# W_ch1 is loaded as bf16 by a casting DMA from the GpSimd queue

## The chip, the cores and the metric

The kernel runs on one core of a Trainium2 chip. A core has engines with an instruction queue each: TensorE (PE, matrix products), VectorE (DVE), ScalarE (ACT), GpSimd (POOL) and SyncE (SP, which here only issues DMAs). Sixteen DMA engines move data between the chip's memory (HBM) and the on-chip buffer (SBUF). Matrix products land in PSUM, which has eight banks. An engine runs its own queue in order; order between engines is made by semaphores only.

The metric is the device time of one execution in microseconds (us). All times inside an execution are given from the start of its span, that is from its first instruction.

## What is computed

```python
kv  = einsum('bhsd,bhse->bhde', k, v)          # 8 batches, 8 heads, 576 rows, 64 columns
o   = einsum('bhsd,bhde->bhse', q, kv)
x   = o / sqrt(mean(o*o, -1) + 1e-6) * g_norm  # heads side by side: x is (8, 576, 512)
a1  = alpha1 * x + beta1
tok = einsum('ts,bsd->btd', w_tok, a1)
u   = x + lam * tok
a2  = alpha2 * u + beta2
ch  = maximum(a2 @ w_ch1, 0) @ w_ch2           # 512 -> 2048 -> 512
out = u + lam * ch
```

All inputs and the output are fp32 in HBM. `w_ch1` is 512 x 2048 and `w_ch2` 2048 x 512, 4 MiB each.

## The kernel before

Every piece of work is first recorded by `P.op(queue, cost, function, r=reads, w=writes)`. `Prog.schedule` then runs the recorded operations through a small planner in Python, with the costs written beside each one, and so fixes the order of each queue; `synchronize` derives the semaphore waits from the reads and writes, and `emit` writes the program. So an edit to one operation, its queue or its planned cost can reorder work on every engine. Two queue names stand for one engine in `queue_of`: "AQ" is a DMA issued from ScalarE's queue.

One batch goes through these stages. Rows of a batch are cut into four chunks of 128 (c0 to c3) and a tail of 64; two batches share one chunk of tails.

- `load_kv`, `load_q` (L324, L330): k, v and q into `kf`, `vf`, `qf`, 1 MiB each, and three tails of 128 KiB. SP issues them, two batches ahead, each as soon as its buffer has been read.
- `round_kv`, `permute_q` (L347, L351, L355): VectorE rearranges them into `kr`, `vr`, `krt`, `vrt`, `qr`.
- `kv_groups` (L366, L369 on TensorE, L389 and L392 to `kvc`) and `qt_groups` (L407, then L414/L420 to `qt`).
- `qkv_groups`, per chunk: L451 (TensorE), the square L459 and root L464 on ScalarE, and on VectorE the sum L461, the reciprocal L467, the product L471 to `xm` (this one frees the chunk's PSUM), L476 to `rt` (bf16) and L480.
- `tok_groups`, per chunk: L496 (TensorE, five matmuls, it needs all five `rt`), L502 (VectorE, adds to `xm`), and two GpSimd operations in a row, L506 to `a1f` and L509 to `a2b`. There is one buffer `a1f`.
- `ut_groups`: transposes L527 of two chunks at a time, and the copy L533 to `a2t` (ScalarE).
- `ch1_groups`: `a2t` times `w1`, L560 on even batches (64 matmuls) and L575 on odd ones (128, with the tails), then the relu L551 to `ht` (ScalarE).
- `ch2_groups`: `ht` times `w2`, L597, then L606 (VectorE) and the store.

The weights are prepared once. `w_tok` goes through L674 and L679 to `wt`. `load_w(i)` for i = 0 to 3 brings a quarter of `w_ch1` into a slot of the fp32 staging buffer `stg` (three slots of 1 MiB) by SP's queue and casts it to bf16 on ScalarE into `w1` (L736); i = 4 to 7 brings a quarter of `w_ch2` into `stg` and multiplies it by `lam` into `w2`, half of it on VectorE and half on GpSimd (both L746). The first four are recorded ahead of batch 0's `qkv_groups`, the last four after batch 1's loads.

Of the kernel before, what the change touches and what calls it, by code (L numbers as in the profile page):

```python
# [10 lines left out]
ACT = mybir.ActivationFunctionType  # L11
# [11 lines left out]
class Op:  # L23
# [3 lines left out]
    def __init__(self, eng, cost, fn, pri, idx):  # L27
        self.eng, self.cost, self.fn, self.pri, self.idx = eng, cost, fn, pri, idx
        self.deps, self.raw = set(), set()
        self.alloc, self.tiles = [], []  # L30
        self.start = self.end = self.pos = None
        self.waits, self.inc, self.lat, self.clock, self.sem = [], False, 0.0, None, None
# [15 lines left out]
class Prog:  # L48
# [5 lines left out]
    def __init__(self, nc, stack):  # L54
        self.nc, self.stack = nc, stack
        self.ops, self.lastw, self.readers = [], {}, {}
        self.ps = stack.enter_context(nc.psum_tensor("ps", [128, 8, 512], F32))
        self.eng = {"PE": nc.tensor, "ACT": nc.scalar, "DVE": nc.vector,
                    "POOL": nc.gpsimd, "SP": nc.sync, "AQ": nc.scalar}
        self.bias = 0  # L60
        self.pe_window = 8

# [112 lines left out]
        self.sequence = sorted(self.ops, key=lambda o: (o.start, o.idx))  # L175

    def queue_of(self, e):
        return "ACT" if e == "AQ" else e

    def synchronize(self):  # L180

# [64 lines left out]
def bass_transnormer_attn__then__resmlp_affine_kernel(  # L246
# [15 lines left out]
    with ExitStack() as stack:  # L262
        P = Prog(nc, stack)

        def sb(name, shape, dt):
            return stack.enter_context(nc.sbuf_tensor(name, shape, dt))
# [14 lines left out]
        qf = sb("qf", [128, NH, 4, DH], F32)  # L281
# [8 lines left out]
        stg = sb("stg", [128, 3, 4, 512], F32)  # L290
# [12 lines left out]
        w1 = sb("w1", [128, 4, FF], BF16)  # L303
# [9 lines left out]
        def dve_us(n, mode=1):  # L313
            return 0.17 + n / 960.0 / mode

        def act_us(n):
            return 0.19 + n / 1200.0
# [269 lines left out]
        def ch2_groups(b):  # L587
# [31 lines left out]
            for c, n in order:  # L619
# [8 lines left out]
            w=["wst"], dma_us=3.0)  # L628
# [3 lines left out]
            w=["wst2"], dma_us=0.5)  # L632
        P.op("SP", 0.6, lambda e: e.dma_start(wst2[0:64, 256:832], moe_w_tok[512:576, :]),
             w=["wst3"], dma_us=0.5)
        for src, dst, key in ((moe_lam, lam_bc, "lam"), (moe_alpha1, e1_bc, "e1"),
# [10 lines left out]
             w=["identb"])  # L646
# [62 lines left out]
        def run(gens):  # L709
            for gen in gens:  # L710
# [14 lines left out]
             r=["wtp"] + [("wtm", i) for i in range(6)], w=["wt", ("sm", 3)])  # L725
# [4 lines left out]

        def load_w(i):
            if i < 4:
                P.op("SP", 0.6, lambda e: e.dma_start(
                    stg[:, i % 3], moe_w_ch1[:, 512 * i:512 * i + 512].rearrange(
                        "(j p) f -> p j f", p=128)), w=[("stg", i % 3)], dma_us=3.2)
                P.op("ACT", act_us(2048), lambda e: e.activation(  # L736
                    w1[:, :, 512 * i:512 * i + 512], stg[:, i % 3], ACT.Identity),
                    r=[("stg", i % 3)], w=[("w1", i)], pri=100)
            else:
                n = i - 4  # L740
                P.op("SP", 0.6, lambda e: e.dma_start(
                    stg[:, i % 3], moe_w_ch2[512 * n:512 * n + 512, :].rearrange(
                        "(j p) c -> p j c", p=128)), w=[("stg", i % 3)], dma_us=3.2)
                for hh in range(2):
                    P.op("POOL" if hh else "DVE", dve_us(1024) * (1 + hh),
                         lambda e, hh=hh: e.tensor_tensor(  # L746
                        out=w2[:, 4 * n + 2 * hh:4 * n + 2 * hh + 2, :],
                        in0=stg[:, i % 3, 2 * hh:2 * hh + 2, :],
                        in1=lam_bc[:, None, :].to_broadcast([128, 2, DM]), op=ALU.mult),
                        r=[("stg", i % 3), "lam"], w=[("w2h", n, hh)])  # L750
                P.lastw[("w2", n)] = P.lastw[("w2h", n, 0)] + P.lastw[("w2h", n, 1)]

        for i in range(4):
            load_w(i)
# [3 lines left out]
        for i in range(4, 8):  # L758
            load_w(i)
# [67 lines left out]
```

## Time and profile before

| what | before |
|---|---|
| time, median of 3 runs | 423.66 us (423.46 to 424.52) |
| the profiled execution: its time | 423.83 us |
| the profiled execution: its span | 422.0 us |
| TensorE busy | 376.5 us (89% of the span), mean granted clock 0.964 |
| VectorE, ScalarE, GpSimd busy | 226.8, 167.5, 120.3 us |
| HBM read, written | 39.37 MB, 9.44 MB |
| ScalarE casts of `w_ch1` (L736) | 4, of 1.90 us each |
| GpSimd multiplications by `lam` (L746) | 4, of 2.35 to 3.32 us |
| VectorE multiplications by `lam` (L746) | 4, of 1.21 to 1.27 us |

The profile is one execution, taken by the hardware profiler. Its page gives the busy time of each engine, the span in 40 slices with the busy share of each in tenths, the chain of work that ended last, and the costliest groups of instructions by line. The same trace can be asked for the instructions in order of time and for the busy times in any stretch. "PEld" is TensorE's loading of weights, "PEclk" the granted TensorE clock as a share of full speed.

### The profile page before, as it was taken

What the parts mean: (1) busy time and instruction counts of PE and PEld (TensorE: products, weight loads), DVE (VectorE), ACT (ScalarE), POOL (GpSimd) and SP (SyncE); (2) the same over time, 40 slices, a digit from 0 to 9 for tenths busy, and PEclk for the clock granted to TensorE, in tenths of its full rate; (3) what the DMA queues carried; (4) which work ended last, traced back from release to release, by engine and by line L of the source; (5) the groups of instructions that cost most, each with busy time, mean ns of one, the idle gap of its engine ahead of it and who ended that gap; (6) DMA issues with size and microseconds to landing.
All of it is one profiled execution on the core that took longest, in us unless ns stands there. A gap on an engine that the chain in (4) does not pass through costs nothing.

```text
span 422.0 us, 5398 instructions
## 1 busy us (share of the span) xinstructions
PE 376.5 (89%) x2193; PEld 227.8 (54%) x2193; DVE 226.8 (54%) x371; ACT 167.5 (40%) x263; POOL 120.3 (29%) x92
## 2 busy tenths in 40 slices
PE   0574755899899999999999999999999999999994
PEld 0563242444677465545775565446774665446642
DVE  3439894995587336862786165743783228620011
ACT  1069142540477025712673135503770157215600
POOL 1000499309300830038003800074007400290000
PEclk9985695999999999999999999999999999999999
DMA  8999999202293019501670139001100201011012
GB/s 241 331 349 302 359 265 351 84 0 99 71 282 85 2 75 263 125 1 61 214 163 2 50 124 284 6 26 51 37 2 0 76 25 25 2 50 51 2 50 75
DMA packets 49128, 49.15 MB, mean 116 GB/s; under 512 B 14608, under 2 KB 39184, under 8 KB 49104
## 3 DMA queue, kind: packets, MB, share of 16 engines
q1 hardware_dynamic: 46672, 46.29, 37.7%
q10 hardware_dynamic: 2432, 2.52, 1.9%
q8 instruction: 17, 0.28, 0.3%
q14 instruction: 7, 0.06, 0.0%
HBM read 39.37 MB, written 9.44 MB: 116 GB/s over the span
## 4 chain that ended last, share of the span: by engine, by line
PE 69%; POOL 12%; DVE 7%; DMA 4%; ACT 3%; issue 2%; POOLq 0%; SPq 0%
PE ps L597 22%; PE ps L575 17%; PE ps L560 12%; POOL a1f L506 6%; POOL a2b L509 6%; PE ps L496 6%; PE ps L451 4%; PE ps L407 4%; DMA qf<-in_q_dram 4%; PE ps L366 2%; PE ps L527 1%; DVE xm L480 1%; DVE xm L502 1%; DVE krt L351 1%; PE ps L674 1%
## 5 line engine op out<-in xcount | busy, mean ns | idle before, releaser
L597 PE MATMUL ps<-w,ht 128*128 128x512 bf16 x576 | 135.3, 379 | 0.0
L506 POOL TENSOR_TENSOR a1f<-xm,a_bc 128x512 f32<-128x512 f32 x32 | 42.8, 1337 | 255.3 <-DVE xm L502 253.5
L551 ACT ACTIVATE ht<-ps 128x640 bf16<-128x640 f32 (+1 forms) x96 | 77.8, 810 | 50.2 <-PE ps L560 25.3
L597 PEld LDWEIGHTS ps<-w,ht 128*128 128x128 bf16 x576 | 54.1, 98 | 57.0 <-DVE xm L502 0.6
L575 PE MATMUL ps<-a2t,w 128*128 128x320 bf16 x512 | 73.0, 299 | 0.0
L606 DVE TENSOR_TENSOR xm<-ps,xm 128x512 f32<-128x512 f32 x32 | 22.1, 690 | 83.1 <-PE ps L597 83.0
L533 ACT ACTIVATE a2t<-ps 128x1024 bf16<-128x1024 bf16 (+1 forms) x20 | 18.8, 938 | 116.8 <-PE ps L527 116.8
L560 PE MATMUL ps<-a2t,w 128*128 128x512 bf16 x256 | 61.2, 388 | 2.6 <-ACT a2t L533 1.1
L575 PEld LDWEIGHTS ps<-a2t,w 128*128 128x128 bf16 x512 | 48.7, 98 | 19.9 <-ACT a2t L533 0.3
L509 POOL TENSOR_TENSOR a2b<-a1f,b_bc 128x512 bf16<-128x512 f32 (+1 forms) x40 | 54.2, 1355 | 3.1
L496 PE MATMUL ps<-rt,wt 128*128 128x512 bf16 x200 | 46.9, 393 | 7.5 <-DVE rt L476 7.5
L560 PEld LDWEIGHTS ps<-a2t,w 128*128 128x128 bf16 x256 | 23.8, 100 | 30.4 <-issue 1.8
L366 PE MATMUL ps<-vr,kr 128*128 128x256 f32 x128 | 26.5, 332 | 13.8 <-DVE vrt L351 13.8
L496 PEld LDWEIGHTS ps<-rt,wt 128*128 128x128 bf16 x200 | 20.0, 100 | 32.5 <-DVE rt L476 7.8
L451 PE MATMUL ps<-kvc,qt 128*128 128x256 f32 x160 | 33.2, 338 | 2.7 <-ACT kvc L392 2.7
L461 DVE TENSOR_REDUCE small<-sq 128x8 f32<-128x512 f32 (+1 forms) x40 | 27.1, 677 | 11.4 <-ACT sq L459 11.3
L502 DVE TENSOR_TENSOR xm<-ps,xm 128x512 f32<-128x512 f32 x32 | 22.0, 690 | 16.9 <-PE ps L496 16.7
L366 PEld LDWEIGHTS ps<-vr,kr 128*128 128x128 f32 x128 | 20.3, 206 | 16.9 <-DVE vrt L351 14.3
L451 PEld LDWEIGHTS ps<-kvc,qt 128*128 128x128 f32 x160 | 25.7, 210 | 6.8 <-ACT kvc L392 3.0
L414 ACT ACTIVATE qt<-ps 128x1024 fp32r<-128x1024 f32 x16 | 16.4, 1024 | 22.3 <-PE ps L407 22.3
L480 DVE SCALAR_TENSOR_TENSOR xm<-e_bc,wsum,xm 128x512 f32<-128x512 f32 x32 | 25.0, 782 | 0.2
L459 ACT ACTIVATE sq<-ps 128x512 f32<-128x512 f32 (+1 forms) x40 | 23.6, 591 | 2.9 <-PE ps L451 2.8
(57 smaller groups left out, 294.6 us busy)
## 6 DMA issues: line engine op xcount, KB each, us to landing
kf<-in_k_dram SPq DMA_DIRECT2D x8, 1024.0 KB, 7.4
qf<-in_q_dram SPq DMA_DIRECT2D x8, 1024.0 KB, 9.6
stg<-in_moe_w_ch_dram SPq DMA_DIRECT2D x8, 1024.0 KB, 10.8
out_dram<-xm SPq DMA_DIRECT2D x32, 256.0 KB, 2.3
vf<-in_v_dram SPq DMA_DIRECT2D x7, 1024.0 KB, 9.0
vf<-in_v_dram ACTq DMA_DIRECT2D x1, 1024.0 KB, 9.8
kft<-in_k_dram SPq DMA_DIRECT2D x8, 128.0 KB, 9.3
qft<-in_q_dram SPq DMA_DIRECT2D x8, 128.0 KB, 9.0
```

The source lines that it names most:

```text
L366: e.matmul(o, flat(kr[:, c, 2 * pr:2 * pr + 2, :]), flat(vr[:, c, u0:u0 + 4, :]), start=(c == 0), stop=False)
L451: m = e.matmul(t.flat()[:, 256 * pr:256 * pr + 256], qt[:, pr, 128 * c:128 * c + 128], kvc[:, pr, :], start=True, stop=True)
L461: P.op("DVE", dve_us(512), lambda e: e.tensor_reduce(out=small[rows, sms], in_=sq[rows, sqs], axis=AX.X, op=ALU.add), r=[("sq", sqs)], w=[ ...
L480: P.op("DVE", dve_us(560), lambda e: e.scalar_tensor_tensor(out=x, in0=e2_bc[rows, :], scalar=wsum[rows, wc:wc + 1], in1=x, op0=ALU.mult, ...
L496: m = e.matmul(t.flat(), wt[:, ws, col:col + 128], rt[:, sc, :], start=(sc == 0), stop=(sc == 4))
L502: P.op("DVE", dve_us(512), lambda e: e.tensor_tensor(out=x, in0=t.flat(rows), in1=x, op=ALU.add), r=[t, xkey(b, c)], w=[xkey(b, c)], pri=-100)
L506: P.op("POOL", pool_us(512), lambda e: e.tensor_tensor(out=a1f[rows, af, :], in0=x, in1=a2_bc[rows, :], op=ALU.mult), r=[xkey(b, c), "a2"] ...
L509: P.op("POOL", pool_us(512), lambda e: e.tensor_tensor(out=a2b[rows, c, :], in0=a1f[rows, af, :], in1=b2_bc[rows, :], op=ALU.add), r=[("a1 ...
L551: P.op("ACT", act_us(n), lambda e: e.activation(dst, src(), ACT.Relu), r=[t], w=key)
L560: m = e.matmul(t.ap()[:, i, :], w1[:, dj, 128 * (fj + i):128 * (fj + i) + 128], a2t[:, dj, 0:512], start=(dj == 0), stop=(dj == 3))
L575: m = e.matmul(t.ap()[:, i, 0:320], w1[:, dj, 128 * fj:128 * fj + 128], a2t[:, dj, 320 * i:320 * i + 320], start=(dj == 0), stop=(dj == 3))
L597: m = e.matmul(t.flat(), ht[:, fj, 128 * c:128 * c + 128], w2[:, fj, :], start=(fj == 0), stop=(fj == 15))
```

## The change

`load_w` for the first four quarters no longer uses `stg` and ScalarE. One DMA, issued from GpSimd's queue under the new name "GQ", reads the fp32 quarter from HBM and writes it as bf16 into its place in `w1`. It is recorded as a reader of `qf`, so it waits until batch 0's q has landed, and batch 1's load into `qf` waits for it. The quarters of `w_ch2` now take the staging slots in the order 0, 1, 2, 0.

```diff
     def queue_of(self, e):
-        return "ACT" if e == "AQ" else e
+        return {"AQ": "ACT", "GQ": "POOL"}.get(e, e)
...
             if i < 4:
-                P.op("SP", 0.6, lambda e: e.dma_start(
-                    stg[:, i % 3], moe_w_ch1[:, 512 * i:512 * i + 512].rearrange(
-                        "(j p) f -> p j f", p=128)), w=[("stg", i % 3)], dma_us=3.2)
-                P.op("ACT", act_us(2048), lambda e: e.activation(
-                    w1[:, :, 512 * i:512 * i + 512], stg[:, i % 3], ACT.Identity),
-                    r=[("stg", i % 3)], w=[("w1", i)], pri=100)
+                P.op("GQ", 1.0, lambda e: e.dma_start(
+                    w1[:, :, 512 * i:512 * i + 512], moe_w_ch1[:, 512 * i:512 * i + 512].rearrange(
+                        "(j p) f -> p j f", p=128)), r=["qf"], w=[("w1", i)], dma_us=3.2)
             else:
                 n = i - 4
                 P.op("SP", 0.6, lambda e: e.dma_start(
-                    stg[:, i % 3], moe_w_ch2[512 * n:512 * n + 512, :].rearrange(
-                        "(j p) c -> p j c", p=128)), w=[("stg", i % 3)], dma_us=3.2)
+                    stg[:, n % 3], moe_w_ch2[512 * n:512 * n + 512, :].rearrange(
+                        "(j p) c -> p j c", p=128)), w=[("stg", n % 3)], dma_us=3.2)
                 for hh in range(2):
                     P.op("POOL" if hh else "DVE", dve_us(1024) * (1 + hh),
                          lambda e, hh=hh: e.tensor_tensor(
                         out=w2[:, 4 * n + 2 * hh:4 * n + 2 * hh + 2, :],
-                        in0=stg[:, i % 3, 2 * hh:2 * hh + 2, :],
+                        in0=stg[:, n % 3, 2 * hh:2 * hh + 2, :],
                         in1=lam_bc[:, None, :].to_broadcast([128, 2, DM]), op=ALU.mult),
-                        r=[("stg", i % 3), "lam"], w=[("w2h", n, hh)])
+                        r=[("stg", n % 3), "lam"], w=[("w2h", n, hh)])
```

The planner, run on the changed list, gives these new orders. GpSimd's queue: the four DMAs, then three of its multiplications by `lam`, then batch 0's L506/L509 pairs, then the fourth multiplication. SP's queue: the first three quarters of `w_ch2` stand where three quarters of `w_ch1` stood; the fourth follows batch 1's k, v and tails; batch 1's q comes only after batch 2's k and v. VectorE: one multiplication by `lam` ahead of the last `rt` of batch 0, one behind it, one after L502 of chunk c1. TensorE: batch 1's L407 and the L451 of its chunks c0 to c3 stand behind batch 0's L560 instead of ahead of it and between; 40 of batch 0's 64 L597 stand ahead of batch 1's L496 instead of 16. From batch 1's first L575 on, the same work is left as before, in nearly the same order.

More of the change, by code (lines that the diff above doesn't have):

```diff
@@ L58, in __init__ @@
         self.eng = {"PE": nc.tensor, "ACT": nc.scalar, "DVE": nc.vector,
-                    "POOL": nc.gpsimd, "SP": nc.sync, "AQ": nc.scalar}
+                    "POOL": nc.gpsimd, "SP": nc.sync, "AQ": nc.scalar, "GQ": nc.gpsimd}
         self.bias = 0
```

## The prediction

> **What bounds the kernel now.** I read the page's slices first, then the busy times by stretch, then the chain of waits in order of time, then single instructions.
>
> ```profile
> PE   0574755899899999999999999999999999999994
> ...
> POOL 1000499309300830038003800074007400290000
> PEclk9985695999999999999999999999999999999999
> DMA  8999999202293019501670139001100201011012
> ```
>
> Each digit is 10.55 us. TensorE is full from the eighth slice on; only the first seven (to 74 us) have room. There the DMA engines are full too, and the granted clock falls to half. GpSimd is idle in slices two to four.
>
> ```profile
> 32.00:45.00 13.00, 5.23 (x22) 4.03 (x22) 12.51 (x27) 9.73 (x14) 0.00 (x0) 0.53 1.12 303
> ...
> 116.00:160.00 44.00, 44.00 (x286) 28.40 (x286) 25.12 (x42) 18.99 (x33) 12.66 (x10) 1.00 0.42 109
> ```
>
> Columns: stretch, length, busy us of PE, PEld, DVE, ACT, POOL, clock, DMA share, GB/s. From 116 us TensorE is at 44.00 of 44.00. From 32 to 45 us the full engine is VectorE, 12.51 of 13.00, and not ScalarE with the casts.
>
> ```profile
> 37.36 1.80 ACT w L736
> ...
> 58.10 0.67 DVE xm L502
> ...
> 59.40 2.23 POOL a1f L506
> 61.63 0.06 POOL w L746
> 61.69 3.18 issue
> 64.87 2.25 POOL a2b L509
> ...
> 67.17 1.05 PE ps L527 x8
> ...
> 69.32 3.61 PE ps L560 x8
> ```
>
> The chain (start, us, what) shows one cast of L736 in it, and further on what holds batch 0's first L560: L502 of chunk c3, then GpSimd's L506, a multiplication by `lam` (L746, 61.6 to 64.9) and L509.
>
> The first L575 of batch 1 starts at 115.94. The work behind it is the same in both kernels, so the end moves as this mark moves: 423.83 (profiled time; 1.83 of it lies outside the span of 422.0) plus the shift. 423.83 is 0.17 above the median. I sum the shift in four steps.
>
> **Step 1, the start of batch 0's L496 (45.09).** The change takes four casts of 1.90 us off ScalarE, 7.6 us. Three lie between 32.9 and 41.8 on the way to `rt`. But VectorE idles 0.49 of those 13 us, so the gain is between 0 and 0.5; I take the one idle stretch of 0.28 that ends with ScalarE's L459. The fourth cast (46.9) has no waiter. Against it, VectorE now makes a multiplication (1.13 from start to next start) ahead of the last `rt` and one L480 (0.73) less: +0.40. Together +0.1.
>
> Then a new collision. GpSimd now multiplies three times between about 31 and 46, where it did nothing.
>
> ```profile
> 54.72 1.76 DVE L480 SCALAR_TENSOR_TENSOR xm<-e_bc,wsum,xm 128x512 f32<-128x512 f32 x1
> ...
> 72.92 4.68 POOL L746 TENSOR_TENSOR w<-stg,lam_bc 128x1024 bf16<-128x1024 f32 x2
> ...
> 75.10 2.78 DVE L351 CAST krt<-kft 64x512 fp32r<-64x512 f32 x1
> ```
>
> A cast of 0.41 us took 2.78 beside a multiplication on GpSimd, an L480 of 0.74 took 1.76 beside L506 and L509. The other way, GpSimd's L506 grew from 1.27 to 2.23 beside VectorE's multiplication. So operations that read SBUF twice, or copy it, exclude GpSimd's. L476, five on this path, has two SBUF inputs like L480. No row shows L476 beside GpSimd. Three multiplications of 2.35: the cost is 0 if each falls on operations with a PSUM input (L502 kept 0.67 beside GpSimd), 7.05 if each holds VectorE whole. I take half, 3.5. Step 1: +3.6.
>
> The DMAs on GpSimd's queue are new. Four issues stand ahead of those multiplications. SP's issues took 0.37 with room and 5.88 (vf at 22.25) without. At 5.88 four end at 18.34 + 23.5 = 41.9, three multiplications at 48.9, against 48.22 for the first L506: 0.7 late, hidden because L502 of c3 decides. So 0 for the issue; above 8 us each it decides. The Trainium skill, "DMA: Bandwidth & Descriptors", section "Anatomy of one DMA — SWDGE (gpsimd) path", calls descriptor generation small and the fixed part of a transfer about 2 us; by it the multiplications would start when `stg` lands and the sum would stay.
>
> **Transfers.** The bytes read stay the same, and the DMA share is 1.0 or more from 4 to 66 us, so only the order moves. Batch 1's k and v now share the engines with seven quarters instead of standing between them. A quarter takes 2.7 us at the 385 GB/s of 46 to 50 us; `w_tok`'s last part landed at 24.2; seven quarters end near 43, kf near 46.5 and vf near 50 at 3.3 each, the tails near 51. VectorE wants them at 52 and later: 0, with some 2 us of cover on vf and 5 on kf. `w1` is wanted at 69, a cover of 26. Batch 1's q now waits on SP behind batch 2's k and v and for all four `w1` DMAs, with only batch 3's k and v due behind it; issued at about 58 + 3.5, landing 10 later (9.8 before) and rearranged by 76, it meets an L407 due at 82: 0.
>
> **Step 2, L496 to L502 of c3.** Before, 13.0 (45.09 to 58.10), 4.49 of it up to L502 of c1. After L502 of c1 the new VectorE order has L502 0.60, multiplication 1.13, kr 1.21, L480 0.73, vr 1.73, L502 0.60, krt 0.81, vrt 0.34, two L480 at 1.69: 10.5 by the durations of this stage. Sum 15.0, so +2.0. Bounds: kr at its 2.31 beside GpSimd adds 1.1; L480 and vr undisturbed take off 2.4.
>
> **Step 3, L502 of c3 to L560.** Before 11.2. The multiplication (61.6 to 64.9, 3.24) is gone from between L506 and L509, and so is VectorE's beside L506. With L502 0.70, L506 and L509 at their usual 1.27 and gaps of 0.1, L527 0.62 and L533 1.03 it is 5.1; with this stage's long ones 8.0. VectorE's next work is L389, with a PSUM input, so I stay near the short end: 5.6, that is -5.6. L560 then starts at 69.3.
>
> **Step 4, L560 to L575.** Before 46.6. After, TensorE makes 64 L560 (0.217 each, 13.9), 16 L407 (1.7), 20 L451 (2.4), 40 L597 (8.6), 26.6 in all, before batch 1's L496. The late L451 cost cover: c3 needs the PSUM that L471 of c0 frees, and square, two sums, reciprocal and product (0.6, 1.3, 0.2, 0.7 and the root 0.3) end 2.35 after TensorE is done with c2; L597 then waits 0.9 for L471 of c1, or 3.7 for c2's. Stalls 3.25 to 6.05; I take 4. Batch 1's `rt` are ready about when the 40 L597 end. From L496 on GpSimd decides: 1.09, L502 0.70, five pairs 13.5, L527 0.40, L533 0.60, 16.4 to 17.0 (before 23.0, bound by TensorE). 30.6 + 16.7 = 47.3: +0.7. The old stage held 2.5 us of half clock (eight L560 in 3.60 and not 1.73, L451 1.42 and not 0.82). Its idle gap was 7.2 us; the new one is near 3.5, and before, the clock fell about 3.8 us into the gap. I charge half, 1.25. Step 4: +2.0.
>
> **Sum.** 3.6 + 2.0 - 5.6 + 2.0 = +2.0, so 425.8.
>
> One rule speaks against the change: the Trainium skill, "SBUF — State Buffer", section "SBUF: two separate sides", says that descriptors from GpSimd's queue can't be written while VectorE runs a two-port copy, and blames stalled DMAs on that. No row here has such a DMA. The copies around the issues are qr (18.34, 1.23 us) and few more until 45; by the rule the `w1` loads start some 1.2 later, and the sum stays, given their cover.
>
> **Rivals.**
> - *GpSimd's multiplications miss VectorE* (other side). For it: most of VectorE's work from 32 to 45 reads PSUM or one SBUF tile. Against: five L476 in 12 us. Place: step 1; price 3.5; with it the gap before L560 shrinks and the clock stays up, 1.25. 425.8 - 4.75 = 421.1. With the clock up, it is faster by over 0.3% when the collisions stay under 1.5 us in all.
> - *Half of both*: one multiplication collides (2.35) and the clock stays up: 425.8 - 1.15 - 1.25 = 423.4, no change that can be told.
> - *The casting transfer takes the engines twice as long a byte.* No row shows one. SP's transfers then run at a third of their pace until about 52: `stg`'s third slot near 53, vf near 60 against a wanted 57.5. L502 of c3, and the end with it, move by some 3: 429. At four times, `w1`'s last quarter comes after 70 and batch 1's q behind it: 436 and more. Against: the packets written are still 1 KiB rows like k's, which moved at about 300 GB/s.
>
> **How the numbers follow.** Forecast 0.42, first rival 0.27, second 0.15, third 0.16. A difference under 0.3% (1.3 us) can't be told from none; 0.05 of the forecast's low end lies there. So faster 0.27, same 0.20, slower 0.53. The range takes in the first rival and the third's near price with some 2 us of step 4's upper stall: 420.8 to 431.0. The forecast's own range is 424 to 428.5.
>
> **What would show it.** L736 gone; L476 or L480 of batch 0 at 1.7 or more beside L746 on GpSimd; L496 near 48.7; L560 near 69 at full clock; L575 near 118. TensorE waiting for `w1` or VectorE for kf would show the third rival; L476 all at 0.68 the first. I am wrong most if GpSimd's four issues take over 8 us each, or if batch 1's q is late.

## The result and the profile after

| | time, median | ratio to the kernel before, 95% interval |
|---|---|---|
| before | 424.09 us | |
| after | 429.33 us (426.76 to 429.77) | 1.0111 [1.0068, 1.0155] |

Both medians are of four executions. The change makes the kernel 1.1% slower. The profiled execution of after took 429.55 us, its span is 427.7. In a second comparison the same program gave 429.77 us and a ratio of 1.0174 [1.0140, 1.0209], because before was a little quicker there (422.72). So the size of the ratio is uncertain by half a per cent from one comparison to the next; its sign is not.

First the slices of the page, as they were read for before (each digit is 10.7 us now):

```profile
PE   0572556979989999999999999999999999999994
...
POOL 1224277002920560019101910065006500190000
PEclk9977666989999999999999999999999999999999
DMA  8999965911196016801490029201100201011012
```

From the eighth slice on (75 us) TensorE is again nearly full but for a dip in the ninth; where the loss lies is read from the marks further down. GpSimd now works in slices two to four, where it was idle. The low clock is still there.

The second view is the chain of waits of after, in order of time (start, us, what), cut to its main pieces:

```profile
39.16 2.81 DVE rt L476
...
45.81 1.13 DVE w L743
...
48.00 3.38 PE ps L496 x9
...
53.14 2.29 DVE kr L347
55.43 1.67 DVE xm L480
...
63.87 0.67 DVE xm L502
...
69.59 12.70 PE ps L560 x47
...
84.50 1.75 PE ps L407 x16
...
94.31 8.44 PE ps L597 x37
102.75 1.09 PE ps L496 x5
...
116.12 2.15 POOL a1f L506
...
118.34 2.15 POOL a2b L509
...
121.79 2.17 PE ps L575 x16
```

L736 and the multiplication between L506 and L509 are gone from it. In their place stand an L476 of 2.81, a multiplication on VectorE (L743, 45.81), then 47 L560 in one block with batch 1's L407 behind them, and at the end L506 and L509 at 2.15 each.

The marks of the prediction, for every kernel that ran (us from the start of the span; "b1" is batch 1; the column L560 to L575 is the difference of its two marks):

| kernel | L496 | L502 c3 | first L560 | L496 b1 | first L575 b1 | L560 to L575 | span | span less L575 |
|---|---|---|---|---|---|---|---|---|
| before | 45.09 | 58.10 | 69.32 | 92.98 | 115.94 | 46.62 | 422.0 | 306.1 |
| after | 48.00 | 63.87 | 69.59 | 102.59 | 121.63 | 52.04 | 427.7 | 306.1 |
| after, again | 48.31 | 64.31 | 69.86 | 102.46 | 121.51 | 51.65 | 427.6 | 306.1 |
| 1: q not held | 48.13 | 65.27 | 70.67 | 92.08 | 113.91 | 43.24 | 420.0 | 306.1 |
| 2: GpSimd late | 45.13 | 61.12 | 67.09 | 97.75 | 119.66 | 52.57 | 425.7 | 306.0 |
| 3: both | 44.02 | 61.16 | 66.56 | 91.08 | 111.15 | 44.59 | 417.3 | 306.2 |
| 3 again | 43.16 | 60.71 | 65.87 | 90.62 | 110.70 | 44.83 | 416.8 | 306.1 |
| 4: 3, VectorE late too | 43.29 | 56.91 | 63.59 | 94.79 | 117.28 | 53.69 | 423.4 | 306.1 |
| 5: before, GpSimd late | 42.79 | 55.80 | 63.33 | 88.89 | 111.03 | 47.70 | 417.1 | 306.1 |
| 6: before, both late | 44.29 | 57.31 | 63.01 | 92.33 | 112.40 | 49.39 | 418.5 | 306.1 |

The last column is the same for all of them: from batch 1's first L575 on, every one of these kernels takes 306.1 us. All that differs has happened by then. In after the mark moved by 5.69 us and the span by 5.7.

### The profile page after: what moved, and what is told of

Its sections match the earlier page's. It is cut to its first block, busy times and chain, and to the rows that moved or that the text cites. A ratio compares the mean times of both kernels' runs of the same rounds, so it can differ in the third digit from the quotient of the medians.

```text
span 427.7 us, 5367 instructions
## 1 busy us (share of the span) xinstructions
PE 374.5 (88%) x2161; PEld 227.4 (53%) x2193; DVE 231.5 (54%) x371; ACT 160.6 (38%) x259; POOL 122.7 (29%) x96
## 3 DMA queue, kind: packets, MB, share of 16 engines
q1 hardware_dynamic: 44560, 42.10, 34.1%
## 4 chain that ended last, share of the span: by engine, by line
PE 70%; POOL 13%; DVE 7%; DMA 4%; issue 3%; ACT 2%; POOLq 0%; SPq 0%
PE ps L597 23%; PE ps L575 16%; PE ps L560 13%; POOL a2b L509 6%; POOL a1f L506 6%; PE ps L496 6%; PE ps L451 4%; DMA qf<-in_q_dram 4%; PE ps L407 4%; PE ps L366 2%; DVE rt L476 1%; PE ps L527 1%; DVE xm L502 1%; DVE xm L480 1%; PE ps L674 1%
## 5 line engine op out<-in xcount | busy, mean ns | idle before, releaser
L597 PE MATMUL ps<-w,ht 128*128 128x512 bf16 x554 | 133.1, 381 | 1.5 <-issue 0.2
L506 POOL TENSOR_TENSOR a1f<-xm,a_bc 128x512 f32<-128x512 f32 x32 | 42.0, 1312 | 230.2 <-DVE xm L502 228.5
L597 PEld LDWEIGHTS ps<-w,ht 128*128 128x128 bf16 x576 | 54.3, 98 | 58.0 <-issue 1.1
L575 PE MATMUL ps<-a2t,w 128*128 128x320 bf16 x512 | 73.0, 299 | 0.0
L560 PE MATMUL ps<-a2t,w 128*128 128x512 bf16 x251 | 60.7, 391 | 1.7 <-ACT kvc L392 1.5
L575 PEld LDWEIGHTS ps<-a2t,w 128*128 128x128 bf16 x512 | 48.7, 98 | 19.9 <-ACT a2t L533 0.6
L496 PE MATMUL ps<-rt,wt 128*128 128x512 bf16 x195 | 44.8, 387 | 13.3 <-DVE rt L476 13.1
L509 POOL TENSOR_TENSOR a2b<-a1f,b_bc 128x512 bf16<-128x512 f32 (+1 forms) x40 | 53.9, 1349 | 3.1
L560 PEld LDWEIGHTS ps<-a2t,w 128*128 128x128 bf16 x256 | 24.3, 100 | 30.0 <-issue 3.4
L496 PEld LDWEIGHTS ps<-rt,wt 128*128 128x128 bf16 x200 | 19.8, 99 | 36.9 <-DVE rt L476 12.9
L451 PE MATMUL ps<-kvc,qt 128*128 128x256 f32 x160 | 30.8, 320 | 4.5 <-ACT kvc L392 2.5
L502 DVE TENSOR_TENSOR xm<-ps,xm 128x512 f32<-128x512 f32 x32 | 22.1, 690 | 17.0 <-PE ps L496 16.9
L366 PEld LDWEIGHTS ps<-vr,kr 128*128 128x128 f32 x128 | 21.4, 217 | 17.2 <-DVE vrt L351 14.6
L451 PEld LDWEIGHTS ps<-kvc,qt 128*128 128x128 f32 x160 | 23.6, 195 | 8.3 <-ACT kvc L392 2.7
L480 DVE SCALAR_TENSOR_TENSOR xm<-e_bc,wsum,xm 128x512 f32<-128x512 f32 x32 | 25.8, 805 | 0.2
L476 DVE TENSOR_TENSOR rt<-xm,e_bc 128x512 bf16<-128x512 f32 x32 | 25.0, 783 | 0.3
```

Source lines behind the costliest of these rows:

```text
L366: e.matmul(o, flat(kr[:, c, 2 * pr:2 * pr + 2, :]), flat(vr[:, c, u0:u0 + 4, :]), start=(c == 0), stop=False)
L451: m = e.matmul(t.flat()[:, 256 * pr:256 * pr + 256], qt[:, pr, 128 * c:128 * c + 128], kvc[:, pr, :], start=True, stop=True)
L476: P.op("DVE", dve_us(512), lambda e: e.tensor_tensor(out=rt[rows, c, :], in0=x, in1=e1_bc[rows, :], op=ALU.mult), r=[xkey(b, c), "e1"], w= ...
L480: P.op("DVE", dve_us(560), lambda e: e.scalar_tensor_tensor(out=x, in0=e2_bc[rows, :], scalar=wsum[rows, wc:wc + 1], in1=x, op0=ALU.mult, ...
L496: m = e.matmul(t.flat(), wt[:, ws, col:col + 128], rt[:, sc, :], start=(sc == 0), stop=(sc == 4))
L506: P.op("POOL", pool_us(512), lambda e: e.tensor_tensor(out=a1f[rows, af, :], in0=x, in1=a2_bc[rows, :], op=ALU.mult), r=[xkey(b, c), "a2"] ...
```

## The experiments

The theory after the result: the casting DMA costs nothing and gains nothing. What the edit changes is the order, by two routes. The first is the record that the DMAs read `qf`: batch 1's q load has to wait for them, SP issues it behind batch 2's k and v, and the planner, which expects q late, puts batch 1's L407 and L451 behind batch 0's L560. The second is that GpSimd's three multiplications by `lam` run early, beside VectorE's work for batch 0. The rival is that the transfer itself does the harm, by its load on the DMA engines or by its issue.

The trace of after speaks against the rival. Its DMA queues (packets, MB, share of 16 engines' time; q0 is the casting queue, whose MB are those written) are:

```profile
q1 hardware_dynamic: 44560, 42.10, 34.1%
q0 software_dynamic: 2112, 2.10, 2.9%
```

2.9% of 427.7 us is 12.4 us of all sixteen engines for the 4.19 MB that the four DMAs read, 338 GB/s; the plain queue takes 145.8 us for 42.10 MB, 289 GB/s. The same 4.19 MB, moved by the plain queue in before, made up about 13.3 us of its time (37.7% of 422.0 us for 46.29 MB there, 145.8 us for 42.10 MB here). So a byte read is not dearer with a cast. The four issues on GpSimd's queue took 1.26, 0.76, 0.77 and 0.76 us, and the last weights landed by 44.6 (last issue at 21.1, at most 23.5 from issue to landing), 25 us before the first L560.

**After, once more**, beside the first three experiments on their chip.

> The changed kernel once more, on the chip of the next three. Both theories: 427 to 430 us, L496 of batch 0 near 48, first L560 near 69.6, first L575 near 121.6. It shows how far single executions spread.

Measured 429.77 us, with every mark within 0.5 us of the first run's. The pattern is fixed.

**1. The q load isn't held.** The DMAs still wait for batch 0's q to land; only batch 1's load no longer waits for them.

```diff
-                P.op("GQ", 1.0, lambda e: e.dma_start(
+                o = P.op("GQ", 1.0, lambda e: e.dma_start(
...
+                P.readers["qf"].remove(o)
```

> The casting DMAs are no longer recorded as readers of qf, so batch 1's q is loaded early again. Theory (the loss is in the order: batch 1's q late, and GpSimd's multiplications in VectorE's way): L407 and L451 of batch 1 lie beside L560 again as before the change, the stretch from the first L560 to the first L575 falls from 52.0 to 46 to 48 us, L496 stays near 48; time 424 to 426.5. Rival (the casting transfer itself is what costs, by slowing the other loads): stays at 428 to 430, the stretch stays over 50.

Measured 421.99 us, 0.9977 [0.9954, 1.0001]: 7.8 us less than after on that chip, and more than was expected. The marks up to the first L560 stay those of after within 1.4 us; the stretch from there to L575 falls from 52.04 to 43.24. So the whole gain is in that stretch: of its 8.80 us, 5.99 are busy time of TensorE (47.28 in after, 41.29 here; the 16 L407 of batch 1 now lie ahead of the stretch) and 2.81 are idle time. Batch 1's q is issued at 44.5 instead of 61.7 (start, us, instruction; after, then experiment 1):

```profile
61.71 0.50 SPq L324 DMA_DIRECT2D qf<-in_q_dram  x1
```

```profile
44.48 1.30 SPq L324 DMA_DIRECT2D qf<-in_q_dram  x1
```

TensorE's order before L560 becomes:

```profile
60.88 1.22 PE L366 MATMUL ps<-vr,kr 128*128 128x256 f32 x4 [2.33 <-DVE vrt L351]
...
63.18 1.91 PE L407 MATMUL ps<-ident,qr 128*128 128x128 f32 x8
64.74 1.20 PE L366 MATMUL ps<-vr,kr 128*128 128x256 f32 x4
...
66.94 1.03 PE L407 MATMUL ps<-ident,qr 128*128 128x128 f32 x8
...
70.67 1.67 PE L560 MATMUL ps<-a2t,w 128*128 128x512 bf16 x7 [0.90 <-ACT a2t L533]
71.99 0.82 PE L451 MATMUL ps<-kvc,qt 128*128 128x256 f32 x4
72.65 1.90 PE L560 MATMUL ps<-a2t,w 128*128 128x512 bf16 x8
```

L407 fills gaps that TensorE has anyway, and each L451 is covered by the L560 behind it. In after the same place reads:

```profile
69.59 12.70 PE L560 MATMUL ps<-a2t,w 128*128 128x512 bf16 x47 [1.52 <-ACT kvc L392]
...
84.34 1.91 PE L407 MATMUL ps<-ident,qr 128*128 128x128 f32 x16
```

Nothing there waits for q: VectorE's copy to `qr` (75.89) and L407 run without idle time before them. It is their places in the queues that are late. The busy times from 70 to 74 us show the other half, for after and then for experiment 1 (busy us of PE, PEld, DVE, ACT, POOL, then clock, DMA share, GB/s):

```profile
70.00:74.00 4.00, 4.00 (x11) 1.47 (x10) 4.00 (x1) 1.09 (x2) 3.07 (x2) 0.50 0.00 0
```

```profile
70.00:74.00 4.00, 3.33 (x18) 1.96 (x20) 3.26 (x2) 3.04 (x6) 3.58 (x2) 1.00 0.14 33
```

From 64 to 70 us TensorE was busy for 2.47 us in after and for 5.03 with L407 in its gaps; then it ran at clock 0.50 in the one and 1.00 in the other, 11 matmuls against 18 (four of them the shorter L451) in the same 4 us.

**2. GpSimd's multiplications late.** Its halves of the multiplications are made to read what batch 0's last L509 writes. q stays held.

```diff
-                        r=[("stg", n % 3), "lam"], w=[("w2h", n, hh)])
+                        r=[("stg", n % 3), "lam"] + [("a2bt", 0)] * hh, w=[("w2h", n, hh)])
```

> GpSimd's multiplications by lam wait until its work on batch 0's chunks is done. Theory: no L476 of batch 0 over 0.8 us, L496 back at 45 to 46, first L560 at 66 to 68, the stretch to L575 stays at 50 to 52; time 425 to 427.5. Rival (casting transfer): L496 stays near 48 or L476 stays slow, as descriptors and transfers are unchanged; time 428 to 430.

Measured 426.84 us, 1.0095 [1.0067, 1.0124], 2.9 us less than after. This time the stretch from L560 on doesn't move (52.57 against 52.04), and the marks before it do: L496 comes at 45.13, which is before's 45.09. The reason is seen in the instructions of VectorE and GpSimd (start, us, instruction). In after, GpSimd's multiplications and the L476 beside them:

```profile
33.63 2.37 POOL L743 TENSOR_TENSOR w<-stg,lam_bc 128x1024 bf16<-128x1024 f32 x1 [3.09 <-DMA stg<-in_moe_w_ch_dram]
39.08 2.35 POOL L743 TENSOR_TENSOR w<-stg,lam_bc 128x1024 bf16<-128x1024 f32 x1 [3.08 <-DMA stg<-in_moe_w_ch_dram]
```

```profile
32.47 0.69 DVE L476 TENSOR_TENSOR rt<-xm,e_bc 128x512 bf16<-128x512 f32 x1
34.76 1.79 DVE L476 TENSOR_TENSOR rt<-xm,e_bc 128x512 bf16<-128x512 f32 x1
39.16 2.81 DVE L476 TENSOR_TENSOR rt<-xm,e_bc 128x512 bf16<-128x512 f32 x1
```

In experiment 2, at the same places:

```profile
31.89 0.69 DVE L476 TENSOR_TENSOR rt<-xm,e_bc 128x512 bf16<-128x512 f32 x1
35.11 0.69 DVE L476 TENSOR_TENSOR rt<-xm,e_bc 128x512 bf16<-128x512 f32 x1
38.42 0.69 DVE L476 TENSOR_TENSOR rt<-xm,e_bc 128x512 bf16<-128x512 f32 x1
```

Two L476 are longer by 1.10 and 2.12 where they meet a multiplication: 3.2 us, against the 2.9 by which L496 came later. The first of the three multiplications (28.18 to 30.54) met no L476: VectorE was waiting for ScalarE's root in most of that time.

**3. Both edits.**

> Both edits together. Theory: the gains add up, L496 at 45 to 46, first L560 at 66 to 68, first L575 at 113 to 116; time 420.5 to 424, level with the kernel before or better. Rival (casting transfer): 427 or more.

Measured 419.84 us, 0.9931 [0.9908, 0.9955], a little below what was expected: 9.9 us less than after, where the single edits gave 7.8 and 2.9, 10.7 together. The two routes are separate and nearly add up. Run again on another chip it gave 419.96 us, 0.9936 [0.9913, 0.9960]:

> The kernel that gave 419.84 us, once more beside the three below. My theory (the loss comes from the order that follows from the edit, not from the casting DMA) needs it to hold: 418.5 to 421.5 us, 0.990 to 0.996 of the kernel before, first L560 near 66.5 us and first L575 near 111. If the gain was a chance of one chip, 422 to 424.

This version beats both kernels. Whether the casting DMA has a part in that, the last two experiments ask.

**4. As 3, with VectorE's halves late as well** (`("a2bt", 0)` for both halves).

> As the run above, and VectorE's halves of the multiplications wait for batch 0's last L509 too. If VectorE's batch 0 chain still pays for them (1.13 us each, two or three of them ahead of L502 of chunk c3), L502 of c3 comes 1 to 3 us earlier than the 61.16 of the run with both edits, and the time is 416 to 419 us. Rival: they are covered there, or now stand in batch 1's chain to rt, on which L575 waits: 419.5 to 423 us, with L496 of batch 1 later than 91.

The rival came true, and worse: 425.50 us, 1.0073 [1.0047, 1.0098]. Chunk c3's L502 does come earlier (56.91), and L560 too, but VectorE now waits 2.50 us for L509, and then both engines multiply at the same time. VectorE, then GpSimd:

```profile
64.51 7.80 DVE L744 TENSOR_TENSOR w<-stg,lam_bc 128x1024 bf16<-128x1024 f32 x3 [2.50 <-POOL a2b L509]
72.33 0.29 DVE L389 TENSOR_TENSOR kvc<-ps,g_bc 64x128 fp32r<-64x128 f32 x1
72.65 2.97 DVE L347 CAST kr<-kf 128x2048 fp32r<-128x2048 f32 x1
```

```profile
64.56 13.27 POOL L744 TENSOR_TENSOR w<-stg,lam_bc 128x1024 bf16<-128x1024 f32 x4
```

Three on VectorE take 7.80 (1.21 each when alone, in the run with both edits) and four on GpSimd 13.27 (2.35 each in after), the last of them beside kr. The last L389 of batch 1 is queued behind them on VectorE, ScalarE's L392 behind that, and TensorE's L451 waits 3.6 us for L392. The stretch from L560 to L575 is 53.69 instead of 44.83.

**5. The kernel before, with GpSimd's multiplications late.** No casting DMA: staging and ScalarE's casts stay.

```diff
-                        r=[("stg", i % 3), "lam"], w=[("w2h", n, hh)])
+                        r=[("stg", i % 3), "lam"] + [("a2bt", 0)] * hh, w=[("w2h", n, hh)])
```

> The kernel before, with fp32 staging and ScalarE casts, and only GpSimd's halves of the multiplications wait for batch 0's last L509. It tells how much of the gain of the run with both edits is the place of these multiplications alone. Theory (order decides, the casting DMA is worth little): the 3.24 us between L506 and L509 of chunk c3 go, first L560 comes 2 to 3.5 us before the 69.32 of the kernel before, and the time is 419 to 422 us. Rival (the casting DMA made the gain, by earlier weights and 7.6 us less on ScalarE): 423 to 425 us.

Measured 420.39 us, 0.9934 [0.9908, 0.9961]. That is the whole gain of experiment 3 (0.9936 beside it) without the change under study. L560 comes 6.0 us earlier than in before, not the 2 to 3.5 expected. Of this, 3.7 lie between L502 of c3 and L560, where the 3.24 us of L746 stood between L506 and L509; now L509 follows L506 at once (GpSimd, chunk c3):

```profile
57.10 2.23 POOL L506 TENSOR_TENSOR a1f<-xm,a_bc 128x512 f32<-128x512 f32 x1
59.41 2.13 POOL L509 TENSOR_TENSOR a2b<-a1f,b_bc 128x512 bf16<-128x512 f32 x1
```

The other 2.3 were already there at L496, and they belong to the single execution and not to the edit: TensorE's and VectorE's orders up to there are the same in both, but batch 0's first sixteen L407 took 1.97 us instead of 3.42 and its q landed 0.3 earlier. Why L407 was quicker isn't settled. 3.7 less the 1.1 by which the stretch from L560 to L575 grew is 2.6, near the 2.7 between the medians (420.39 against 423.13). The marks are of one execution, of 418.92 us, 1.5 below the median; the verdict rests on the ratios.

**6. The kernel before, with both halves late.**

> The kernel before, with both halves of the multiplications waiting for batch 0's last L509. Theory: as the run above or a little better, 418 to 422 us, and the casting DMA's own worth, read against the run that has it with the same late halves, is under 3 us. Rival (the casting DMA made the gain): 423 to 425 us; or w2, finished later, holds L597: over 425 us.

Measured 419.20 us, 0.9919 [0.9890, 0.9948], the lowest of all, though not to be told from 3 and 5. Here only two of VectorE's multiplications start at once (4.52 us for the two), and all four L389 stand ahead of them, so that the wait of experiment 4 for L392 is not there. The stretch from L560 on is still 1.7 us longer than in experiment 5.

So the casting DMA with its order put right (3) and staging with the same late multiplications (5) give the same time to within their intervals of about 0.25% each way. The planner makes different orders for the two (L560 at 65.87 and 63.33, L575 at 110.70 and 111.03), so this bounds what the casting DMA is worth in orders of this kind; a run with one and the same order for both wasn't made. The other pair with the same late multiplications, 4 and 6, missed what was expected of it (under 3 us): the version with the casting DMA is 6.3 us slower (425.50 against 419.20). The rows of the two put this down to the order, in which three multiplications stand ahead of VectorE's last L389 in 4 and none in 6; that the casting DMA has no part in these 6.3 us is argued from the rows and not shown by a run. The new order of the slots in `stg` was not tried by itself either.

## Why the prediction was right and where its size was off

The forecast of slower was right and 429.33 lies in the range of 420.8 to 431.0, but 3.5 us above 425.8 and just outside the forecast's own 424 to 428.5. Its steps, against the marks of after:

| step | predicted | measured |
|---|---|---|
| 1, start of L496 | +3.6 | +2.91 |
| 2, L496 to L502 of c3 | +2.0 | +2.86 |
| 3, L502 of c3 to L560 | -5.6 | -5.50 |
| 4, L560 to L575 | +2.0 | +5.42 |
| sum | +2.0 | +5.69 |

- **Step 1** held in mechanism and nearly in size: two of the three multiplications met an L476 and cost 3.2 us where half of 7.05 had been taken. That half came so near is luck, as nothing in the working said which of them would meet one. Experiment 2 shows the cost by taking them away; L496 then falls back to 45.13 (batch 0's first L407 took 3.2 to 3.4 us in these three executions, so the marks can be compared), and the casts that ScalarE lost gave nothing, as the term of +0.1 had it. The issues of the DMAs cost 3.5 us of GpSimd's queue in all, at a time when it waited for `stg` anyway. The rule weighed there, of "SBUF — State Buffer", section "SBUF: two separate sides" in the Trainium skill, could show in the first issue: it began at 18.42, during VectorE's copy to `qr` (18.14 to 19.37), and took 1.26 us against 0.76 for the others. That can be the rule or a first issue's own cost; in either case it is 0.5 us under cover.
- **Transfers** at 0: no wait of TensorE for `w1` and none of VectorE for batch 1's `kf` or `vf` is in the trace.
- **Step 2** was 0.9 too small. The bound named for it came true: kr took 2.29 beside GpSimd, vr 2.28 where 1.73 had been put in, and the first L480 1.75 where 0.73 had been. From L502 of c1 on this made 12.47 instead of 10.5; against it, L502 of c1 came 3.40 after L496 instead of 4.49.
- **Step 3** held to 0.1 us. That the first three steps together are only 0.3 off is partly luck, since the errors of steps 1 and 2 cancel.
- **Step 4** is the term that was mis-sized, by 3.4 us. Two parts of it failed. "I charge half, 1.25" for the half clock: none was saved. 47 L560 took 12.70 us instead of 10.2 at the 0.217 used, 2.5 us, at a clock of 0.50 from 70 to 74; TensorE had been hardly busier ahead of L560 than in before (2.47 of 6.00 us from 64 to 70, against 1.72). In the second execution of the same program the 47 took 11.49, 1.3 over, so this part differs from one execution to the next. And "five pairs 13.5" for GpSimd: they took 15.85 (104.64 to 120.49), since the last L506 and L509, at 2.14 each, ran beside VectorE's next kr and vr (115.13 and 117.85); two more were 1.60. 1.25 and 2.35 make 3.6. The stalls agree only in the sum: 33.0 from L560 to batch 1's L496, less 26.6 of work and 2.5 of clock, leaves 3.9 where 4 had been taken, but TensorE was idle for 2.5 of the 33.0. In the rest, matmuls took longer than the durations used, some of them at a clock that fell to 0.50 a second time (92 to 94 us), after L451's wait of 1.90 for L471.
- **The late q** was looked at and priced by the wrong question. "It meets an L407 due at 82: 0" is true of the wait and misses the cost: the place at 82 is already the consequence of q's being late. (The prediction did name a late q among the two things that would make it most wrong.) Experiment 1 puts the price of the order that follows from it at 7.8 us, the largest single effect of the change. The prediction had it in step 4, as late L451 and a shorter gap, but counted only what the new order cost against before's, not that before's order hid more.
- **The rivals.** The first (the multiplications miss VectorE, 421.1) falls by the L476 of 1.79 and 2.81, the second (half of both) by two collisions and a clock that stayed down. The third (a dearer casting transfer, 429) has the nearest time, by luck, but not its cause: q0's 2.9%, the weights 25 us early, no wait for them. Experiment 1 keeps the casting transfers and is 7.8 us quicker.

## What to carry to other kernels

Where a planner orders the work, ask of each read or write that an edit records what else it holds back: here a single recorded reader of a buffer cost 7.8 us, more than anything that the transfer itself did. Moving work to an idle engine is free only if it doesn't slow what now runs beside it (here an L476 of 0.69 us took 1.79 and 2.81); price it by a row in which the two are seen together. And before a gain is put down to a change, run the kernel before with only the order changed: here late multiplications alone gave all of it.

## What the runs showed of the hardware

- A DMA that casts fp32 to bf16 took no more engine time for a byte read than the plain ones: 12.4 us of sixteen engines for 4.19 MB (338 GB/s) against 289 GB/s, and against about 13.3 us for the same bytes in before. An issue of it took GpSimd 0.76 us, the first 1.26.
- VectorE's and GpSimd's multiplications of two SBUF operands slow each other when they run at once: from 1.21 to 2.60 us on average on VectorE (7.80 for three, experiment 4). GpSimd's went from 2.35 to 3.32 (13.27 for four), beside these and then beside the casts kr and vr, which took 2.97 and 3.37.
- The clock of TensorE went with what it had done shortly before. In the ten executions, where it had been busy for 0.98 to 2.82 us of the 6.00 ahead of the first L560, the mean clock in the 3.00 behind L560's start was 0.50 to 0.60 (before, after twice, experiments 2, 5 and 6); where for 3.38 to 4.73 us, it was 1.00 (experiments 1, 3 twice and 4).
